# Key-feature sums through one-pass products, and due times shifted by line

## The chip, the cores and the metric

The kernel runs on one core of a Trainium2 chip. The metric is the device time of one execution in microseconds; the time before is the median of three runs, 858.32 us (857.91 to 858.6).

## What is computed

Random-feature attention over q, k, v (4 batches, 8 heads, 576 tokens, head size 64, 128 features) is followed by two feed-forward layers on 2304 tokens of width 512 (inner width 2048), all in fp32:

```python
k_p, q_p = phi(k * scale), phi(q * scale)      # exp of a projection, 128 features
kv  = einsum('bhsm,bhsd->bhmd', k_p, v)
z   = sum(k_p, axis=2)                         # sums of the key features, one row of 128 per head
num = einsum('bhsm,bhmd->bhsd', q_p, kv)
den = einsum('bhsm,bhm->bhs', q_p, z) + 1e-06
x = (num / den) as (2304, 512)
x = leaky_relu(x @ w_in, 0.01) @ w_out
h = x @ w2_in;  out = (h * clip(h + 3, 0, 6) / 6) @ w2_out
```

The change touches z and how it reaches the tokens' denominators.

## The kernel before

**Stages.** Attention works on pairs of heads: 4 batches times 4 pairs give 16 key units (`K_unit`), each followed by query units. Batch 0 stands ahead of everything (`Q_first`, to about 47 us). The other three batches, 12 key units, are woven into the first feed-forward layer (to about 310 us). The second layer runs from there to the end; its products are made by a scheme with fewer multiplications (L1202 for the first product, L1099 for the second).

**Products.** Large products are made of operands cut into a high part and a remainder, both of the type fp32r, in three passes (`mm3`, L520 to L522; also L1099 and L1202). Attention's small products are plain fp32. The scores (L778) use 64 of the array's 128 rows; the products with v (L845) and the numerators (L1002) use 64 of its columns; the transposes (L971, L852) use all of it.

**Sums of the key features.** For batches 1 to 3, `K_unit` adds the 4 blocks of tokens of each head on GpSimd or VectorE (L861 to L866, here L509 and L865 in the profile), which leaves a tile `zr` of 128 partitions by 2 heads by 128 features. One fp32 product with a tile of ones (L869) sums over the partitions and gives every partition the sums; ScalarE or VectorE copies them back to `zr` (L871). The denominators are then taken per token by VectorE against `zr` (L945).

**What sets the order.** Nothing waits at run time to be placed: while the program is built, `Graph.run` plays a list scheduler. Each operation (`g.op`) names the engines that could do it with a cost for each, and a due time; the scheduler takes the one that can start first by its own clock, and among near ones the one that is due first. PE's attention work has three modes, S (64 rows), N (64 columns) and F (whole array), and the constants `WAIT`, `FOLLOW` and `MATE` say how long such work is held back to stand next to its like. The tables `MOVE_A`, `MOVE_W` and `MOVE_R` shift due times of attention units, weights and unpacked weights in steps of 100 ns. Where the scheduler sees PE without work in the first stage it puts in products that nobody reads (`keep_warm`, L1400), 16 of them at the start.

**Tiles.** `h` has 5 buffers (and 6 more in the first stage), `hh` is a small one for a unit of one block, `zr` has 6, `junk` takes an output that nobody reads, `g` is the cut left operand of L1099 (3 buffers, and a fourth, `late_g`, in the second layer).

Of the kernel before, what the change touches and what calls it, by code (L numbers as in the profile page):

```python
# [8 lines left out]
F32 = mybir.dt.float32  # L9
# [28 lines left out]
PACE = 2.215  # L38
WAIT = {"S": 3500.0, "N": 1700.0, "F": 1300.0}
FOLLOW = 200.0  # L40
MATE = 20.0
TURN = {("M", "S"): 193.0, ("M", "N"): 92.0, ("S", "M"): 205.0, ("N", "M"): 158.0, ("F", "S"): 193.0, ("F", "N"): 97.0, ("S", "F"): 175.0,
# [11 lines left out]
ATT = [None, (32000.0, 132000.0), (132e3, 170000.0), (182e3, 244000.0), (220e3, 260000.0)]  # L54
MOVE_A = [[-202, 0, -28, 44, -92, 0, -54, 8, -3],
# [4 lines left out]
MOVE_W = [-30, 30, -3, 103, 35, 68, 105, 97, 0, 53, 7, 110, 0, 28, -99, 0, -14, 35, 50, 3, -192, -42, 60, -500, 41, 288, -17, -51, -123, -27, 96, 0]  # L60
MOVE_R = [24, 10, -139, 36, 14, -45, -29, -31, -102, 77, -175, -71, -46, -9, -4, 0, 59, 11, -146, 0, -17, -36]
RAW = (142000.0, 302000.0)
# [33 lines left out]
class Graph:  # L96
# [17 lines left out]
    def __init__(self):  # L114
        self.ops = []
        self.fifo = {}
        self.todo = {}

    def op(self, alts, rd=(), wr=(), due=0.0, also=(), late=False, lag=0.0, mode="F", after=0.0):
        o = Op()  # L120
        o.phase, o.second = Buf.NOW, Buf.SECOND
        self.todo[o.phase] = self.todo.get(o.phase, 0) + 1
        o.alts, o.due, o.seq, o.lazy = alts, due, len(self.ops), LAZY if late else lag
        o.slack = self.slack if alts[0][0] == "pe" else 0.0
# [242 lines left out]
def attn_moe_kernel(ctx: ExitStack, tc: tile.TileContext, qT, kT, qn, kn, v1, om2, w1i, w1o, w2i, w2o, out):  # L367
# [20 lines left out]
    def many(n, name, *specs, pool=const):  # L388
        return [tuple(sb(f"{name}{i}_{j}", *s, pool=pool) for j, s in enumerate(specs)) for i in range(n)]

    def duo(t, later=0):
# [16 lines left out]
        "sq": many(3, "sq", ([128, 9, 1],), pool=misc),  # L408
        "junk": many(1, "junk", ([128, 2, 128], BF16), pool=misc),
        "hb": [],  # L410
# [10 lines left out]
        "h": many(5, "h", ([128, 512],), pool=right),  # L421
        "hh": many(2, "hh", ([128, 128],), pool=right),
        "ht": many(2, "ht", ([128, 512],), pool=right),
        "tq": many(1, "tq", ([128, 2, 512],), pool=right),
    }
    slots.update(late)
# [60 lines left out]
    wn = sb("wn", [128, 128])  # L487
    ones = sb("ones", [128, 128])
    zero = sb("zero", [128, 128], F32R)
    slots["den"] = many(3, "den", ([128, 4, 1],), ([128, 4, 1],))  # L490
    three = sb("three", [128, 8], pool=misc)[:, 0:1]
    point5 = sb("point5", [128, 32], pool=misc)[:, 0:1]

# [263 lines left out]
    def scores(f, half, xsrc, nsrc, due, nh=1):  # L757
# [8 lines left out]
        ps = [Ps(g.use) for _ in cols]  # L766
        hs = [Buf("h" if c > 1 else "hh") for c in cols]

# [36 lines left out]
    def K_unit(b, hp, due):  # L805
# [49 lines left out]
        for e in range(2):  # L855
            Z = lambda e=e: zr.tiles[0][:, e]

            for i, m in ((1, 256), (0, 128)):
# [7 lines left out]
                 rd=[ht], wr=[(zr, e)], due=due + 3e3)  # L866
        flat = lambda: zr.tiles[0].rearrange("p h m -> p (h m)")
        pz = Ps(g.use)
        g.op([("pe", 435.0, lambda: nc.tensor.matmul(pz.tiles[0][:, 0:256], lhsT=ones, rhs=flat(), start=True, stop=True))],  # L869
             rd=[zr], wr=[pz], due=due + 3.5e3)  # L870
        g.op(copy_alts(flat, lambda: pz.tiles[0][:, 0:256], 256, True), rd=[pz], wr=[zr], due=due + 4e3)  # L871

# [49 lines left out]
    def Q_unit(grp, b, hps, f, half, s0, col0, o, due):  # L922
# [14 lines left out]
        for bank, (h, c) in enumerate(zip(hs, cols)):  # L937
# [4 lines left out]
            def dn(h=h, den=den, jk=jk, heads=heads):  # L942
                for q, (k, _, e) in enumerate(heads):
                    for e, r in [(0, slice(0, 64)), (1, slice(64, 128))] if e is None else [(e, slice(0, 128))]:
                        nc.vector.tensor_tensor_reduce(out=jk.tiles[0][r, q % 2], in0=h.tiles[0][r, q * 128:q * 128 + 128],  # L945
                                                       in1=zr[k].tiles[0][r, e], scale=1.0, scalar=M * EPS, op0=ALU.mult,
                                                       op1=ALU.add, accum_out=den.tiles[0][r, q])
# [437 lines left out]
    with tc.manual_schedule():  # L1385
        nc.vector.memset(three, 3.0)
        nc.gpsimd.memset(ones, 1.0)
        nc.vector.memset(point5, 0.5)
        nc.scalar.activation(slots["nm"][0][0][:, 0], three, AF.Exp)
        nc.sync.dma_start(wn, om2)  # L1390
        nc.gpsimd.memset(zero.bitcast(F32), 0.0)
        make_identity(nc, ident)
        nc.vector.tensor_scalar(out=wn, in0=wn, scalar1=-scale, scalar2=None, op0=ALU.mult)

        def keep_warm(n):
            for _ in range(n):
                nc.tensor.matmul(banks[-1][0][:, 0:384], lhsT=zero[:, 0:128],  # L1400
                                 rhs=zero[:, None, 0:128].to_broadcast([128, 3, 128]), start=True, stop=True)

        g.keep_warm = keep_warm
        g.run(slots, len(banks) - 1, phase, [phase2, phase3, phase4, phase5])
# [81 lines left out]
```

## Time and profile before

| | |
|---|---|
| median of 3 runs | 858.32 us |
| the profiled execution | 858.16 us, span 856.4 us |
| PE busy | 849.2 us of the span |
| DVE, ACT, POOL busy | 658.2, 510.1, 205.0 us |
| DMA | 226 GB/s on average |

The span is the time from the first to the last instruction; the execution's own time is 1.8 us more. PE is TensorE with its products, PEld its loading of weights, DVE is VectorE, ACT is ScalarE, POOL is GpSimd, SP is the engine that issues most DMAs. A product's time in the rows is a latency: two products that follow each other overlap, so the step from one start to the next is what a product occupies.

### The profile page before, as it was taken

The page shows a single profiled execution, that of the slowest core. Times are in us where ns is not written, and L with a number is a line of the kernel's source. Part 1 is how long each engine was busy: PE and PEld are TensorE (multiplying, and loading weights), DVE is VectorE, ACT ScalarE, POOL GpSimd, SP SyncE. Part 2 cuts the span into 40 slices and gives each one's busy share as a digit, 9 for nine tenths or more (in the row PEclk, how much of TensorE's full clock was granted, in tenths as well). Part 3 has the DMA queues.
Part 4 walks back from the last instruction along what each step waited for, and adds up shares of the span by engine and source line. Part 5 has one row for each costly group of instructions (what it writes and reads, how often), then busy time and mean ns, then how long its engine had stood idle before and what let it go on. Part 6 is the DMA issues. An engine that isn't in the chain of part 4 may idle for free.

```text
span 856.4 us, 18060 instructions
## 1 busy us (share of the span) xinstructions
PE 849.2 (99%) x6281; PEld 778.1 (91%) x6281; DVE 658.2 (77%) x1714; ACT 510.1 (60%) x1163; POOL 205.0 (24%) x288
## 2 busy tenths in 40 slices
PE   9999999999999999999999999999999999999998
PEld 8988888889878878888888889999999999999998
DVE  6988998977996855656789757887678779868765
ACT  6988886886887555544654455544543554445432
POOL 0245464334124321000100002122002222422110
PEclk9999999999999999999999999999999999999999
DMA  8666653775757306999878829977896784686451
GB/s 325 221 205 197 216 179 119 244 228 194 234 186 249 126 25 226 321 332 326 327 266 291 284 74 298 314 284 229 297 328 209 237 271 151 193 287 216 155 148 44
DMA packets 110250, 193.83 MB, mean 226 GB/s; under 512 B 13520, under 2 KB 46416, under 8 KB 110160
## 3 DMA queue, kind: packets, MB, share of 16 engines
q1 hardware_dynamic: 110016, 192.55, 68.1%
q8 instruction: 50, 0.82, 0.4%
q14 instruction: 40, 0.33, 0.1%
q10 hardware_dynamic: 144, 0.13, 0.1%
HBM read 148.60 MB, written 44.04 MB: 225 GB/s over the span
## 4 chain that ended last, share of the span: by engine, by line
PE 95%; DVE 2%; ACT 1%; POOL 1%; issue 0%; DVEq 0%; POOLq 0%
PE bank L1099 19%; PE bank L1202 18%; PE bank L520 15%; PE bank L522 15%; PE bank L521 15%; PE bank L778 4%; PE bank L1002 2%; PE bank L845 2%; PE bank L971 1%; PE bank L823 1%; PE bank L897 1%; PE bank L1400 1%; PE bank L869 1%; PE bank L798 0%; PE bank L772 0%
## 5 line engine op out<-in xcount | busy, mean ns | idle before, releaser
L501 ACT COPY late_u<-bank 128x256 f32<-128x256 f32 (+1 forms) x94 | 36.4, 387 | 78.0 <-PE bank L1202 73.8
L1041 DVE TENSOR_TENSOR g<-bank,g 128x512 fp32r<-128x512 f32 (+1 forms) x80 | 50.4, 634 | 39.7 <-ACT g L501 38.7
L1099 PE MATMUL bank<-w,g 128*128 128x256 f32 x612 | 80.8, 275 | 0.0
L1099 PEld LDWEIGHTS bank<-w,g 128*128 128x128 f32 x612 | 74.4, 192 | 0.1
L1202 PE MATMUL bank<-w,late_w 128*128 128x256 f32 x546 | 72.8, 275 | 0.0
L753 ACT ACTIVATE h<-bank,nm 128x128 f32<-128x128 f32 x228 | 63.6, 389 | 10.8 <-DVE nm L747 9.2
L1039 ACT ACTIVATE bank<-bank 128x512 f32<-128x512 f32 (+1 forms) x80 | 44.5, 556 | 41.8 <-PE bank L522 41.7
L1202 PE MATMUL bank<-x,late_w 128*128 128x256 f32 x540 | 69.3, 275 | 0.0
L520 PE MATMUL bank<-x,w 128*128 128x512 f32 (+1 forms) x180 | 67.5, 375 | 0.2 <-DVE g L1041 0.2
L520 PE MATMUL bank<-g,w 128*128 128x512 f32 (+1 forms) x180 | 67.3, 374 | 0.0
L1202 PEld LDWEIGHTS bank<-w,late_w 128*128 128x128 f32 x546 | 67.0, 192 | 0.2
L1202 PEld LDWEIGHTS bank<-x,late_w 128*128 128x128 f32 x540 | 64.9, 192 | 0.2
L522 PE MATMUL bank<-x,w 128*128 128x512 f32 (+1 forms) x180 | 64.6, 359 | 0.0
L521 PE MATMUL bank<-x,w 128*128 128x512 f32 (+1 forms) x180 | 64.5, 358 | 0.0
L521 PE MATMUL bank<-g,w 128*128 128x512 f32 (+1 forms) x180 | 64.5, 358 | 0.0
L522 PE MATMUL bank<-g,w 128*128 128x512 f32 (+1 forms) x180 | 64.5, 358 | 0.0
L741 DVE TENSOR_REDUCE nm<-bank 128x4 f32<-128x512 f32 (+2 forms) x76 | 47.5, 655 | 17.5 <-PE bank L778 15.0
L1099 PE MATMUL bank<-second_w,g 128*128 128x256 f32 x453 | 59.9, 275 | 0.0
L1099 PEld LDWEIGHTS bank<-second_w,g 128*128 128x128 f32 x453 | 55.2, 192 | 0.0
L501 ACT COPY u<-bank 128x256 f32<-128x256 f32 (+1 forms) x59 | 24.0, 409 | 50.0 <-PE bank L1202 30.8
L956 POOL TENSOR_TENSOR h<-h,den 128x512 f32<-128x512 f32 (+2 forms) x32 | 32.9, 1034 | 83.2 <-DVE den L951 52.4
L504 DVE TENSOR_TENSOR g<-xr,g 128x512 fp32r<-128x512 f32 (+1 forms) x55 | 36.7, 667 | 11.8 <-ACT g L501 10.7
(392 smaller groups left out, 2377.5 us busy)
## 6 DMA issues: line engine op xcount, KB each, us to landing
late_w<-in SPq DMA_DIRECT2D x207, 256.0 KB, 4.2
in<-late_w SPq DMA_DIRECT2D x64, 256.0 KB, 3.8
third_w<-in SPq DMA_DIRECT2D x49, 256.0 KB, 4.2
wst<-w2i SPq DMA_DIRECT2D x16, 512.0 KB, 4.5
wst<-w2o SPq DMA_DIRECT2D x16, 512.0 KB, 4.8
x_t<-late_w SPq DMA_DIRECT2D x12, 512.0 KB, 4.4
v<-v SPq DMA_DIRECT2D x14, 330.0 KB, 3.5
wst<-w1i SPq DMA_DIRECT2D x9, 512.0 KB, 3.7
```

Source lines behind the costliest of these rows:

```text
L501: return [("act", c_act(n, psum), lambda: nc.scalar.copy(dst(), src())), dve if psum else dve + (True,)]
L504: return [("dve", c_dve(n), lambda: nc.vector.tensor_tensor(out=dst(), in0=src(), in1=hi().bitcast(F32), op=ALU.subtract), True), ("pool", ...
L520: nc.tensor.matmul(o, lhsT=ah, rhs=bh, start=start, stop=False)
L521: nc.tensor.matmul(o, lhsT=al, rhs=bh, start=False, stop=False)
L522: nc.tensor.matmul(o, lhsT=ah, rhs=bl, start=False, stop=stop)
L741: g.op([("dve", c_dve(c * 128), lambda raw=raw, n_=n_: nc.vector.tensor_reduce(out=n_()[:, :, 0], in_=raw(), axis=AX.X, op=ALU.min))], rd= ...
L753: nc.scalar.activation(h.tiles[0][:, q * 128:q * 128 + 128], raw()[:, q], AF.Exp, bias=nm.tiles[0][:, q], scale=-1.0)
L778: nc.tensor.matmul(ps[e].tiles[0][:, at:at + 128], lhsT=src.tiles[0][r, k * one + i * 128:k * one + i * 128 + 128], rhs=wn[r], start=True, ...
L1039: g.op([("act", c_act(n, True), lambda: nc.scalar.activation(P(), P(), AF.Prelu, alpha=0.01))], wr=[p], due=d)
L1041: g.op([("dve", c_dve(n), lambda: nc.vector.tensor_tensor(out=G1(), in0=P(), in1=G0().bitcast(F32), op=ALU.subtract))], rd=[p, (gg, 0)], w ...
L1099: nc.tensor.matmul(acc[bank].tiles[0][:, half * 256:half * 256 + 256], lhsT=src.tiles[x][:, q * 128:q * 128 + 128], rhs=woven(w[k].tiles[y ...
L1202: nc.tensor.matmul(R[r](), lhsT=w[x], rhs=m[y], start=start and k == n == 0, stop=k == 1 and n == 2, skip_group_check=True)
```

## The change

Four things are done together.

1. The fp32 product with ones (L869) becomes two one-pass products. `zr` is rounded to fp32r in a new tile `zz` (first half, ACT or DVE), the remainder is subtracted into its second half (DVE or POOL), and both are multiplied with ones of the type fp32r into one bank. The moving operand is read in the interleaved order that `woven` gives, so the copy back to `zr` puts the two heads in order again.
2. `ones` is now of type fp32r and also feeds the products of `keep_warm`; the tile `zero` and its fill are gone.
3. `junk` shrinks, `hh` is gone: units of one block take a buffer of `h`.
4. The tables and constants of the order are new, and a table `MOVE_S` shifts due times by the line that calls `g.op`.

```diff
-WAIT = {"S": 3500.0, "N": 1700.0, "F": 1300.0}
-FOLLOW = 200.0
-MATE = 20.0
+WAIT = {"S": 1900.0, "N": 1800.0, "F": 1250.0}
+FOLLOW = 60.0
+MATE = 380.0
...
-MOVE_A = [[-202, 0, -28, 44, -92, 0, -54, 8, -3],
+MOVE_A = [[-369, -68, -26, 0, -91, 0, -38, 0, -69],
...
+MOVE_S = [3, 25, -11, -195, -112, 3, 2, -19, 11, 4, 0, -32, -38, 7, -14, -26, 0, -10, -215, 43, -6, 31, -17, 3, -88, 56, -2, 17, 23, 0, 87, -19, 0, 0, 0, -48, 36, 71, -28, -115, -64, 93, -98, 1, 13, -97, 0, 80, -16, 352, 55, 0, 0, 1, -28, 15, -160, -124, 22, 22, 30, -14, 64, -21, -50, 128, 1, 90, -30, -114, 20, 15, 0, 27, 6, -60, 8, -38, 0, 34, -126, 0, 11]
...
+        self.sites = {}
...
+        site = self.sites.setdefault(sys._getframe(1).f_lineno, len(self.sites))
+        due += MOVE_S[site] * 100.0 if site < len(MOVE_S) else 0.0
...
-        "junk": many(1, "junk", ([128, 2, 128], BF16), pool=misc),
+        "junk": many(1, "junk", ([128, 1, 128], BF16), pool=misc),
...
-        "hh": many(2, "hh", ([128, 128],), pool=right),
...
+        "zz": many(1, "zz", ([128, 512], F32R), pool=right),
...
-    ones = sb("ones", [128, 128])
-    zero = sb("zero", [128, 128], F32R)
+    ones = sb("ones", [128, 128], F32R)
...
-        hs = [Buf("h" if c > 1 else "hh") for c in cols]
+        hs = [Buf("h") for _ in cols]
...
+        zz = Buf("zz")
+        Zh, Zl = (lambda e=e: zz.tiles[0][:, e * 256:e * 256 + 256] for e in range(2))
+        g.op([("act", c_act(256), lambda: nc.scalar.copy(Zh(), flat())), ("dve", 320.0, lambda: nc.vector.tensor_copy(Zh(), flat()), True)],
+             rd=[zr], wr=[(zz, 0)], due=due + 3.2e3)
+        g.op([("dve", c_dve(256), lambda: nc.vector.tensor_tensor(out=Zl(), in0=flat(), in1=Zh().bitcast(F32), op=ALU.subtract), True),
+              ("pool", c_pool(256), lambda: nc.gpsimd.tensor_tensor(out=Zl(), in0=flat(), in1=Zh().bitcast(F32), op=ALU.subtract))],
+             rd=[zr, (zz, 0)], wr=[(zz, 1)], due=due + 3.2e3)
         pz = Ps(g.use)
-        g.op([("pe", 435.0, lambda: nc.tensor.matmul(pz.tiles[0][:, 0:256], lhsT=ones, rhs=flat(), start=True, stop=True))],
-             rd=[zr], wr=[pz], due=due + 3.5e3)
-        g.op(copy_alts(flat, lambda: pz.tiles[0][:, 0:256], 256, True), rd=[pz], wr=[zr], due=due + 4e3)
+        def rep():
+            for n, x in enumerate((Zh, Zl)):
+                nc.tensor.matmul(pz.tiles[0][:, 0:256], lhsT=ones, rhs=woven(x()), start=n == 0, stop=n == 1)
+        g.op([("pe", 224.0, rep)], rd=[zz], wr=[pz], due=due + 3.5e3)
+        back = lambda: zr.tiles[0].rearrange("p h m -> p m h")
+        g.op(copy_alts(back, lambda: pz.tiles[0][:, 0:256].rearrange("p (m h) -> p m h", h=2), 256, True), rd=[pz], wr=[zr], due=due + 4e3)
...
-        nc.gpsimd.memset(ones, 1.0)
+        nc.gpsimd.memset(ones.bitcast(F32), 1.0)
...
-        nc.gpsimd.memset(zero.bitcast(F32), 0.0)
...
-                nc.tensor.matmul(banks[-1][0][:, 0:384], lhsT=zero[:, 0:128],
-                                 rhs=zero[:, None, 0:128].to_broadcast([128, 3, 128]), start=True, stop=True)
+                nc.tensor.matmul(banks[-1][0][:, 0:384], lhsT=ones,
+                                 rhs=ones[:, None].to_broadcast([128, 3, 128]), start=True, stop=True)
```

In the changed kernel's lines, L869 is L883, L865 is L869, L1099 is L1115, L520 to L522 are L524 to L526, L1202 is L1218 and L509 is L513; the new copy is L874 and the new subtraction L877.

**GpSimd, first of the 12 sums.** Names are out<-in; `h1`, `h2` are the key features of the two heads, `ht1` the tail of the batch, `w..` weights being prepared. Before, then the change:

```order
L509 TENSOR_TENSOR h1_0_146<-h1_0_146 128x256
L509 TENSOR_TENSOR h2_0_147<-h2_0_147 128x256
L509 TENSOR_TENSOR zr4_0_138<-h1_0_146 128x128
L509 TENSOR_TENSOR zr4_0_138<-h2_0_147 128x128
L865 TENSOR_TENSOR zr4_0_138<-zr4_0_138,ht1_0_153 64x128 x2
L505 TENSOR_TENSOR w10_93<-wt0_0_110,w10_93 128x512
```

```order
L513 TENSOR_TENSOR h1_0_146<-h1_0_146 128x256
L513 TENSOR_TENSOR h2_0_147<-h2_0_147 128x256
L513 TENSOR_TENSOR zr4_0_138<-h1_0_146 128x128
L513 TENSOR_TENSOR zr4_0_138<-h2_0_147 128x128
L869 TENSOR_TENSOR zr4_0_138<-zr4_0_138,ht1_0_151 64x128 x2
L877 TENSOR_TENSOR zz0_0_153<-zr4_0_138,zz0_0_153 128x256
```

The subtraction of the remainder stands on GpSimd behind the sums, and it does so in all 12 units; its input, the rounded half, comes from ScalarE in 11 of them and from VectorE in one.

**PE, the same sum's product.** Before, then the change (`x..`, `g..` are cut operands of the first layer):

```order
L520 MATMUL bank6_182<-x0_101,w8_91 128x512
L521 MATMUL bank6_182<-x0_101,w8_91 128x512
L522 MATMUL bank6_182<-x0_101,w8_91 128x512
L869 MATMUL bank5_181<-zr4_0_138,ones_186 128x256
L520 MATMUL bank6_182<-x1_102,w8_91 128x512
```

```order
L524 MATMUL bank3_178<-g2_107,w5_88 128x512
L525 MATMUL bank3_178<-g2_107,w5_88 128x512
L526 MATMUL bank3_178<-g2_107,w5_88 128x512
L883 MATMUL bank0_175<-zz0_0_153,ones_185 128x256 x2
L524 MATMUL bank7_182<-g2_107,w5_88 128x512
```

Two instructions stand for one. Between the last product with v of this unit (L845, which frees `h` for the sums) and the product with ones, the order before has 21 one-pass products of 512 columns, the order now 27.

**PE, about 820 us, where the last group's products begin.** Before, `late_g1` is used, refilled and used again:

```order
L1099 MATMUL bank6_182<-w8_91,late_g1_0_0_3824 128x256 x3
L1099 MATMUL bank1_177<-third_w0_0_0_1615,g2_107 128x256 x3
L1099 MATMUL bank3_179<-w4_87,g1_106 128x256 x3
L1099 MATMUL bank4_180<-w3_86,late_g1_0_0_3824 128x256 x3
L1099 MATMUL bank0_176<-w6_89,late_g1_0_0_3824 128x256 x3
L1099 MATMUL bank3_179<-w7_90,late_g1_0_0_3824 128x256 x3
```

Now, at the same place, first products of the next group (L524 to L526) stand between:

```order
L1115 MATMUL bank4_179<-w5_88,g1_106 128x256 x3
L1115 MATMUL bank1_176<-w1_84,g1_106 128x256 x3
L524 MATMUL bank6_181<-x0_101,late_w0_3_0_3921 128x256
L525 MATMUL bank6_181<-x0_101,late_w0_3_0_3921 128x256
L526 MATMUL bank6_181<-x0_101,late_w0_3_0_3921 128x256
L1115 MATMUL bank7_182<-w8_91,g1_106 128x256 x3
L524 MATMUL bank6_181<-x1_102,late_w0_2_0_3920 128x256
L525 MATMUL bank6_181<-x1_102,late_w0_2_0_3920 128x256
L526 MATMUL bank6_181<-x1_102,late_w0_2_0_3920 128x256
L1115 MATMUL bank4_179<-w6_89,late_g1_0_0_3922 128x256 x3
```

Before, 6 products stand between the last use of the buffer's old content and the first use of its new one; now 18 do (three L524 to L526 ahead of the first row shown are the rest of them).

## Rows read from the trace of the kernel before

**Rows 1.** The page: engines' busy time, and the chain that ended last, by engine

```profile
PE 849.2 (99%) x6281; PEld 778.1 (91%) x6281; DVE 658.2 (77%) x1714; ACT 510.1 (60%) x1163; POOL 205.0 (24%) x288
...
PE 95%; DVE 2%; ACT 1%; POOL 1%; issue 0%; DVEq 0%; POOLq 0%
```

**Rows 2.** Stretches: length, then PE, PEld, DVE, ACT, POOL busy, clock, DMA

```profile
68.00:140.00 72.00, 71.77 (x424) 60.53 (x423) 65.75 (x135) 58.57 (x126) 36.90 (x38) 1.00 0.58 188
...
300.00:480.00 180.00, 180.00 (x879) 154.05 (x879) 127.54 (x272) 97.90 (x194) 15.74 (x16) 1.00 0.79 269
```

**Rows 3.** Timeline of PE around the first product with ones: start, length, instruction

```profile
69.62 0.38 PE L522 MATMUL bank<-x,w 128*128 128x512 f32 x1
69.83 0.59 PE L869 MATMUL bank<-zr,ones 128*128 128x256 f32 x2
70.08 0.57 PE L520 MATMUL bank<-x,w 128*128 128x512 f32 x1
70.48 0.38 PE L521 MATMUL bank<-x,w 128*128 128x512 f32 x1
```

**Rows 4.** Timeline of PE: one-pass products of 256 columns

```profile
152.41 0.28 PE L521 MATMUL bank<-x,w 128*128 128x256 f32 x1
152.52 0.28 PE L522 MATMUL bank<-x,w 128*128 128x256 f32 x1
```

**Rows 5.** Timeline of PE around the fourth product with ones

```profile
131.66 0.38 PE L522 MATMUL bank<-g,second_w 128*128 128x512 f32 x1
132.04 0.70 PE L869 MATMUL bank<-zr,ones 128*128 128x256 f32 x2
...
132.80 0.38 PE L521 MATMUL bank<-g,second_w 128*128 128x512 f32 x1
```

**Rows 6.** Timeline of PE: into the 64-row scores and out again

```profile
143.36 0.38 PE L522 MATMUL bank<-g,second_w 128*128 128x512 f32 x1
143.67 0.94 PE L778 MATMUL bank<-wn,xT 64*128 64x128 f32 x12
144.54 0.88 PE L971 MATMUL bank<-ident,h 128*128 128x128 f32 x6
```

**Rows 7.** Groups by form, ACT and POOL: count, busy us, mean ns, idle before

```profile
L501 ACT CAST late_w<-late_u 128x256 fp32r<-128x256 f32 x9 | 3.6, 405 | 0.8 <-DMA in<-late_w 0.5 <-DVE late_u L508 0.3
...
L505 POOL TENSOR_TENSOR x<-xr,x 128x256 fp32r<-128x256 f32 x5 | 3.7, 742 | 0.1
```

**Rows 8.** Timeline of PE, 717 to 719.6 us

```profile
717.51 1.35 PE L1099 MATMUL bank<-w,g 128*128 128x256 f32 x9
719.01 0.60 PE L1099 MATMUL bank<-third_w,g 128*128 128x256 f32 x3
```

**Rows 9.** Timeline, 821.5 to 825.5 us: the refill of `late_g`, then PE's next products

```profile
822.89 0.51 ACT L501 CAST late_g<-xr 128x384 fp32r<-128x384 f32 x1 [2.31 <-PE bank L1099]
...
823.44 0.84 DVE L504 TENSOR_TENSOR late_g<-xr,late_g 128x384 fp32r<-128x384 f32 x1
...
823.46 0.38 PE L1099 MATMUL bank<-w,late_g 128*128 128x256 f32 x1
...
824.34 1.16 PE L1099 MATMUL bank<-w,late_g 128*128 128x256 f32 x8 [0.50 <-DVE late_g L504]
```

**Rows 10.** Timeline of the first stage: the start, and a VectorE operation beside GpSimd

```profile
0.87 0.20 POOL L1391 MEMSET zero<- 128x128 f32 x1
...
1.13 5.49 PE L1400 MATMUL bank<-zero 128*128 128x384 f32 x16 [1.13 <-POOL zero L1391]
...
39.05 0.68 DVE L560 SCALAR_TENSOR_TENSOR wst<-wt,wst 128x512 uint32<-128x512 uint32 x1
...
44.74 1.29 POOL L505 TENSOR_TENSOR w<-first_wt,w 128x512 fp32r<-128x512 f32 x1
44.77 1.37 PEld L1400 LDWEIGHTS bank<-zero 128*128 128x128 f32 x8
44.80 1.67 PE L1400 MATMUL bank<-zero 128*128 128x384 f32 x8
...
45.52 1.06 DVE L560 SCALAR_TENSOR_TENSOR wst<-first_wt,wst 128x512 uint32<-128x512 uint32 x1
...
46.50 0.41 DVE L906 TENSOR_TENSOR u<-bank,den 128x256 f32<-128x256 f32 x1
...
46.97 0.66 PE L915 MATMUL bank<-ident,u 128*128 128x128 f32 x4 [0.51 <-DVE u L906]
```

More of the change, by code (lines that the diff above doesn't have):

```diff
@@ L1 @@
+import sys
 from contextlib import ExitStack
@@ L54 @@
 ATT = [None, (32000.0, 132000.0), (132e3, 170000.0), (182e3, 244000.0), (220e3, 260000.0)]
-MOVE_A = [[-202, 0, -28, 44, -92, 0, -54, 8, -3],
[4 rows of a table removed]
-MOVE_W = [-30, 30, -3, 103, 35, 68, 105, 97, 0, 53, 7, 110, 0, 28, -99, 0, -14, 35, 50, 3, -192, -42, 60, -500, 41, 288, -17, -51, -123, -27, 96, 0]
-MOVE_R = [24, 10, -139, 36, 14, -45, -29, -31, -102, 77, -175, -71, -46, -9, -4, 0, 59, 11, -146, 0, -17, -36]
+MOVE_A = [[-369, -68, -26, 0, -91, 0, -38, 0, -69],
[4 rows of a table added]
+MOVE_W = [-95, 4, -18, 11, 0, 63, 106, 113, -32, 76, 0, 0, -47, -18, 0, 20, -2, 7, 35, -114, -233, 48, 108, -735, -22, 116, 113, 71, -62, -128, 0, 8]
+MOVE_R = [8, 43, -131, 71, -104, 0, -42, -39, -108, 115, 0, 103, -15, 99, -26, 0, -18, -83, -20, -282, 0, 69]
+MOVE_S = [3, 25, -11, -195, -112, 3, 2, -19, 11, 4, 0, -32, -38, 7, -14, -26, 0, -10, -215, 43, -6, 31, -17, 3, -88, 56, -2, 17, 23, 0, 87, -19, 0, 0, 0, -48, 36, 71, -28, -115, -64, 93, -98, 1, 13, -97, 0, 80, -16, 352, 55, 0, 0, 1, -28, 15, -160, -124, 22, 22, 30, -14, 64, -21, -50, 128, 1, 90, -30, -114, 20, 15, 0, 27, 6, -60, 8, -38, 0, 34, -126, 0, 11]
 RAW = (142000.0, 302000.0)
@@ L487, in attn_moe_kernel @@
     wn = sb("wn", [128, 128])
-    ones = sb("ones", [128, 128])
-    zero = sb("zero", [128, 128], F32R)
+    ones = sb("ones", [128, 128], F32R)
     slots["den"] = many(3, "den", ([128, 4, 1],), ([128, 4, 1],))
     three = sb("three", [128, 8], pool=misc)[:, 0:1]
-    point5 = sb("point5", [128, 32], pool=misc)[:, 0:1]
+    point5 = sb("point5", [128, 8], pool=misc)[:, 0:1]
     def Ps(use):
@@ L944, in dn @@
                     for e, r in [(0, slice(0, 64)), (1, slice(64, 128))] if e is None else [(e, slice(0, 128))]:
-                        nc.vector.tensor_tensor_reduce(out=jk.tiles[0][r, q % 2], in0=h.tiles[0][r, q * 128:q * 128 + 128],
+                        nc.vector.tensor_tensor_reduce(out=jk.tiles[0][r, 0], in0=h.tiles[0][r, q * 128:q * 128 + 128],
                                                        in1=zr[k].tiles[0][r, e], scale=1.0, scalar=M * EPS, op0=ALU.mult,
```

8 rows, old and new, of the table MOVE_A are left out of this document.

## The prediction

> **What bounds the kernel now.** I read the page first, for who is busy and which chain ended last. PE is busy for 849.2 of 856.4 us and makes up 95% of the chain [rows 1]. A busy PE is not yet a PE without gaps, because a product's length in the rows is a latency; so the view by stretches came next, and then the timeline of PE, where the step from one start to the next is what a product occupies. In the stretches PE shows no idle time from 300 to 480 us and 0.2 us from 68 to 140 [rows 2]. In the timeline the steps are 0.21 us for 512 columns [rows 3] and 0.11 us for 256 [rows 4], and after 50 us they leave these values in a few places only. So the kernel's time is the sum of PE's steps, plus a few waits, plus a first stage (to about 47 us) in which PE is held up by a chain through ScalarE and VectorE, plus a short end. Work that leaves PE shortens the kernel one for one, if nothing else becomes late.
>
> **The product with ones.** Before, it stands between two products of 512 columns. From its start at 69.83 to the start of the second product behind it at 70.48 are 0.65 us; one 512-column step of 0.21 is in that, so the fp32 product occupies 0.44 us [rows 3]. Now two one-pass products of 256 columns stand there, at 0.11 each [rows 4]: 0.22 us, with the same interleaved reading that those of rows 4 have. The saving is a little over 0.21 us, 12 times: **-2.5 us**. What could make it less is a loading of ones that isn't hidden; each 256-column product of rows 4 loads its own weights too and keeps its step, so I take no such cost.
>
> **What it adds elsewhere.** Per sum one rounding of 256 columns, on ScalarE in 11 of 12 cases, 0.41 us by the nearest row, and one subtraction of 256 columns on GpSimd, 0.74 us by the nearest row [rows 7]. Together that is 4.5 us on ScalarE (11 of them) and 8.9 us on GpSimd, over some 220 us. Neither is on PE's path by itself. But the chain from the last product with v to the product with ones becomes longer by 0.41 + 0.74 = 1.15 us and two hand-overs. It is covered if the order leaves PE that much more to do in between. It does: counted in the order at the steps of rows 3 and 4, PE's work between the two is 4.8 to 8.5 us before and 6.1 to 9.4 now; the first has 6 more products of 512 columns, 1.3 us. Only the third has 6.1 us in both. Before, one of the twelve made PE wait, the fourth: it started 0.38 us after its predecessor instead of 0.21, and its own stretch took 0.76 instead of 0.65, together 0.28 us lost [rows 5]. If the third now does what the fourth did, the extra link costs at most 1.15 us there; if the fourth is on time (9.4 us of work now), 0.28 come back. I take 0 for both.
>
> **Changes of the array's shape.** A step into the 64-row scores is 0.31 us where 0.21 would do, 0.10 lost, and the way out costs some more [rows 6]. That is what `FOLLOW`, `MATE` and `WAIT` trade in. Counted over both orders, scores stand in 34 runs before and now, and 64-column products in 28; but pairs of the two that stand side by side go from 15 to 14, so there is one more change of shape in all, 109 to 110. **+0.2 us**, between 0.1 and 0.3.
>
> **The order late in the program.** Two places lose time to PE waiting on its own refills. At 717.51 nine products of 256 columns take 1.50 us to the next start, where nine steps are 1.01: 0.49 lost [rows 8]. At 823.46 one product takes 0.88 us instead of 0.11: 0.77 lost [rows 9]. The second is plain to read: `late_g1` may be refilled only when the products that read it are through; the cast on ScalarE starts at 822.89 and takes 0.51, the subtraction on VectorE starts at 823.44 and takes 0.84, and PE has just 6 products, 0.67 us, in between. In the order now 18 products, 2.0 us, stand there, and the cast and the subtraction need 0.51 + 0.84 = 1.35. At the place that answers to 717 us, products of the next group are likewise put between. I take both waits as gone: **-1.3 us**, between -1.6 (smaller ones beside them vanish too) and 0 (they turn up at the next refill).
>
> **The first stage.** The fill of `zero`, 0.20 us, goes, and the opening run of 16 unread products, which waited for it until 1.13 us, can start up to 0.2 us earlier [rows 10]. There are 39 unread products instead of 37, at about 0.2 us each by the run of 8 at 44.80 [rows 10]; they stand where the scheduler saw nothing to do, and I cost them at nothing, since PE would wait there anyway; without that cover they are +0.4. The products at the chain's end keep their order, and the VectorE operation at 45.52 (L560) still stands ahead of the last multiplication of that stage (L906 at 46.50), on which the last transposes wait (L915 at 46.97) [rows 10]. I take 0, between -0.6 and +0.8.
>
> **The middle, 50 to 310 us.** Every attention unit stands at another place than before. The waits there are small: I found none larger than the 0.28 at the fourth sum [rows 5], and four or five such, about 1 us in all, are the most that can be won; new ones may come. I take 0, between -1 and +1.5. DMAs are issued in another order too; the core's 16 engines are 0.58 to 0.79 busy in the stretches that I read [rows 2], and I cost that at nothing.
>
> **Sum.** The profiled execution took 858.16 us: 858.16 - 2.5 + 0.2 - 1.3 = 854.56. The median of the runs is 0.16 above that execution, less than the terms are known to. I predict **854.6 us**.
>
> **The rivals.**
> - *Only the products count.* The late waits stay or come back at other refills: 858.16 - 2.5 + 0.2 = 855.9. For it: such waits depend on 0.1 us, and VectorE's queue can delay a refill with enough PE work beside it. Against it: 2.0 us stand where 1.35 are needed.
> - *The saving is eaten by new waits in the middle.* The longer chain to the product with ones misses its place a few times, or other units wait: the third at 1.15 us and as much again at others, 855.9 + 1.2 = 857.1, no change that can be told. For it: VectorE is busy for 65.75 of 72 us from 68 to 140 [rows 2], so there is little room. Against it: eleven of twelve distances grew.
> - *GpSimd's new work blocks VectorE: slower.* A VectorE operation that takes 0.68 us (39.05) takes 1.06 at 45.52, where a subtraction on GpSimd from 44.74 for 1.29 overlaps its start [rows 10]. So 12 more GpSimd subtractions of 0.74 can push VectorE back by up to 8.9 us in all; where its room is used up (6.25 us are left from 68 to 140, with four of the sums), PE waits for the cut operands `g`. With all of it landing on PE, 854.6 + 8.9 = 863.5; it decides from 5.3 us landed, which turns -3.6 into +1.7. The Trainium skill, "SBUF — State Buffer", section "SBUF: two separate sides", says that GpSimd and VectorE share a port pair under an exclusive lock, held for a whole instruction; by that rule the loser stands still for as long as the other still needs. The trace agrees: the 0.38 us added to L560 lie inside GpSimd's 1.29. Against it: each block lasts under a microsecond, and where VectorE is fullest PE was idle for 0.2 us in all [rows 2].
> - *The one-pass products don't keep their step*, because ones are loaded in a way that rows 4 don't show, and take as long as the fp32 one: 854.6 + 2.5 = 857.1.
>
> **How the numbers follow.** My forecast, up to 0.9 us to either side of 854.6: 0.50. Only the products count, 855.4 to 856.6: 0.28. Better than forecast, because waits in the middle and the first stage go as well (854.6 - 1 - 0.6 = 853.0 and about): 0.06. Saving eaten or steps not kept, within 0.2% of 858.3 (1.7 us, about what a measurement of this kernel can tell from no change): 0.13. Slower: 0.03. So faster 0.84, same 0.13, slower 0.03. The range is 853.0 to 857.3: down to where the middle and the first stage both pay, up over the eaten saving; outside are some 0.05 below and 0.09 above.
>
> **What would show it.** In the changed kernel's profile: 24 products on L883 as pairs, 0.22 us from the first start to the product behind the pair; about 849.2 - 3.6 us of PE busy time; no gap over 0.3 us on PE near 715 and 820 us; VectorE's share not above 78%. The prediction is wrong if PE waits for `zz` (L877) by name more than once or twice, if VectorE's operations beside L877 grow and PE waits behind them, or if the first stage ends more than 0.8 us away from where it did (the last L915 started at 46.97 us).

## The result, and the profile after

The changed kernel takes 863.73 us, the median of 4 runs (863.36 to 865.65), where the kernel before takes 858.29: a ratio of 1.0065, with a 95% interval of 1.0052 to 1.0079. It is slower by 5.4 us. The forecast was 854.6, faster. The profiled execution took 865.65 us, span 863.9, the longest of the four, so it shows about 2 us more loss than the median.

The places that the prediction named (the pair, the two late waits) came as it said; PE's busy time fell by 0.4 us, not by 3.6. From the page of the changed kernel, busy time, and the chain that ended last by engine and by line:

```profile
PE 848.8 (98%) x6283; PEld 776.0 (90%) x6283; DVE 658.7 (76%) x1720; ACT 520.6 (60%) x1183; POOL 206.3 (24%) x285
...
PE 78%; DVE 8%; DMA 5%; ACT 4%; issue 2%; POOL 1%; SPq 0%; DVEq 0%; ACTq 0%; POOLq 0%
PE bank L1115 19%; PE bank L1218 17%; PE bank L524 11%; PE bank L526 11%; PE bank L525 11%; DMA wst<-w2i 2%; PE bank L782 2%; DVE junk L961 2%; ACT h L757 1%; DMA xn<-qn 1%; DVE nm L745 1%; DVE wst L564 1%; DVE g L1057 1%; PE bank L827 1%; 
```

The chain is 78% PE where it was 95% [rows 1]; the rest of it runs through other engines. PE itself is idle for 15.1 us of the span (863.9 less 848.8), where it was for 7.2 (856.4 less 849.2). Timeline of PE, the first product with ones and the place that answers to [rows 8]:

```profile
70.74 0.38 PE L526 MATMUL bank<-g,w 128*128 128x512 f32 x1
70.96 0.38 PE L883 MATMUL bank<-zz,ones 128*128 128x256 f32 x2
71.18 0.38 PE L524 MATMUL bank<-g,w 128*128 128x512 f32 x1
...
718.34 1.17 PE L1115 MATMUL bank<-second_w,g 128*128 128x256 f32 x9
719.35 1.50 PE L1115 MATMUL bank<-second_w,late_g 128*128 128x256 f32 x12
720.69 1.17 PE L1115 MATMUL bank<-second_w,g 128*128 128x256 f32 x9
```

The pair takes 0.22 us from its start to the next product, where the fp32 product took 0.44 [rows 3]. Nine products take 1.01 us to the next start (718.34 to 719.35), as nine steps should, where [rows 8] had 1.50; the wait of [rows 9] has no counterpart either. The loss is in the middle. The view by stretches, 80 to 340 us (length, then PE, PEld, DVE, ACT, POOL busy, clock, DMA share, GB/s), before:

```profile
80.00:340.00 260.00, 259.77 (x1856) 218.69 (x1855) 210.03 (x635) 192.66 (x494) 96.67 (x118) 1.00 0.57 183
```

The same of the change, and whom PE waited for there:

```profile
80.00:340.00 260.00, 251.91 (x1814) 210.90 (x1813) 206.33 (x616) 189.95 (x483) 102.87 (x131) 1.00 0.53 168
```

```profile
PE bank L883 <- ACT h L757: 1.6, 1, 1.6
PE bank L782 <- DVE g L1057: 1.5, 1, 1.5
PE bank L526 <- DVE g L1057: 1.2, 1, 1.2
PE bank L524 <- ACT xr L505: 0.8, 1, 0.8
PE bank L524 <- DVE g L1057: 0.8, 1, 0.8
```

PE is idle for 8.1 us there in place of 0.2, in eleven waits, nearly all for ScalarE and VectorE; the five longest are shown. The first, at the seventh product with ones, is not one for `zz`: that sum's `zz` was finished 4.5 us before the product started. One small wait for `zz` there is, at the third sum, and this view leaves it out. The second product of the pair needs the end of the subtraction, and the next product starts 0.70 us after the start of the pair, where the same place takes 0.32 without the subtraction (115.51 to 115.83 in the run without it, below):

```profile
116.80 0.73 POOL L877 TENSOR_TENSOR zz<-zr,zz 128x256 fp32r<-128x256 f32 x1 [0.52 <-ACT zz L874]
117.10 0.86 PE L883 MATMUL bank<-zz,ones 128*128 128x256 f32 x2
117.80 0.38 PE L524 MATMUL bank<-g,second_w 128*128 128x512 f32 x1
```

VectorE's busy time in this stretch is *lower* than before, with 616 instructions in place of 635; over the whole span it is the same (658.7 and 658.2 us). What it does in its idle time shows in its timeline. Before, reductions of one query unit against `zr`, each with a reading of its accumulator:

```profile
215.19 0.28 DVE L945 CUSTOM_DVE_ANT_0 junk<-h,zr 128x128 bf16<-128x128 f32 x1
215.40 0.08 DVE L945 DVE_READ_ACCUMULATOR2_ANT den<- 128x1 f32 x1
215.40 0.29 DVE L945 CUSTOM_DVE_ANT_0 junk<-h,zr 128x128 bf16<-128x128 f32 x1
215.61 0.08 DVE L945 DVE_READ_ACCUMULATOR2_ANT den<- 128x1 f32 x1
215.63 0.29 DVE L945 CUSTOM_DVE_ANT_0 junk<-h,zr 128x128 bf16<-128x128 f32 x1
```

And in the change:

```profile
218.16 0.28 DVE L961 CUSTOM_DVE_ANT_0 junk<-h,zr 128x128 bf16<-128x128 f32 x1
218.37 0.08 DVE L961 DVE_READ_ACCUMULATOR2_ANT den<- 128x1 f32 x1
218.48 0.29 DVE L961 CUSTOM_DVE_ANT_0 junk<-h,zr 128x128 bf16<-128x128 f32 x1
218.70 0.08 DVE L961 DVE_READ_ACCUMULATOR2_ANT den<- 128x1 f32 x1
218.93 0.29 DVE L961 CUSTOM_DVE_ANT_0 junk<-h,zr 128x128 bf16<-128x128 f32 x1
```

Before, a reduction starts 0.21 us after the last one, before that one's 0.28 are over. Now it starts 0.32 or 0.45 after it, always behind its end, and so do all 102 that follow another directly. The change cut `junk`, the output that nobody reads, from two halves used in turn to one. It made room, and the prediction passed over it. This theory came only after the first four runs, which all kept the short `junk`.

### The profile page after: what moved, and what is told of

It reads as the page before. It is cut to its first block, busy times and chain, and to the rows that moved or that the text cites. A ratio compares the mean times of both kernels' runs of the same rounds, so it can differ in the third digit from the quotient of the medians.

```text
span 863.9 us, 18057 instructions
## 1 busy us (share of the span) xinstructions
PE 848.8 (98%) x6283; PEld 776.0 (90%) x6283; DVE 658.7 (76%) x1720; ACT 520.6 (60%) x1183; POOL 206.3 (24%) x285
## 4 chain that ended last, share of the span: by engine, by line
PE 78%; DVE 8%; DMA 5%; ACT 4%; issue 2%; POOL 1%; SPq 0%; DVEq 0%; ACTq 0%; POOLq 0%
PE bank L1115 19%; PE bank L1218 17%; PE bank L524 11%; PE bank L526 11%; PE bank L525 11%; DMA wst<-w2i 2%; PE bank L782 2%; DVE junk L961 2%; ACT h L757 1%; DMA xn<-qn 1%; DVE nm L745 1%; DVE wst L564 1%; DVE g L1057 1%; PE bank L827 1%; PE bank L913 1%
## 5 line engine op out<-in xcount | busy, mean ns | idle before, releaser
L1115 PE MATMUL bank<-w,g 128*128 128x256 f32 x594 | 81.9, 275 | 0.0
L1218 PE MATMUL bank<-x,late_w 128*128 128x256 f32 x558 | 74.7, 275 | 0.0
L1115 PEld LDWEIGHTS bank<-w,g 128*128 128x128 f32 x594 | 73.9, 192 | 0.0
L1218 PE MATMUL bank<-w,late_w 128*128 128x256 f32 x540 | 71.1, 275 | 0.0
L1218 PEld LDWEIGHTS bank<-x,late_w 128*128 128x128 f32 x558 | 68.5, 192 | 0.3 <-ACT late_u L505 0.2
L524 PE MATMUL bank<-x,w 128*128 128x512 f32 (+1 forms) x180 | 66.6, 370 | 1.8 <-ACT xr L505 0.8
L1218 PEld LDWEIGHTS bank<-w,late_w 128*128 128x128 f32 x540 | 66.1, 192 | 0.5 <-ACT late_u L505 0.2
L524 PE MATMUL bank<-g,w 128*128 128x512 f32 (+1 forms) x180 | 66.1, 367 | 0.0
L526 PE MATMUL bank<-x,w 128*128 128x512 f32 (+1 forms) x180 | 64.8, 360 | 0.1
L526 PE MATMUL bank<-g,w 128*128 128x512 f32 (+1 forms) x180 | 64.5, 358 | 0.0
L1115 PE MATMUL bank<-second_w,g 128*128 128x256 f32 x438 | 60.0, 275 | 0.0
L1115 PEld LDWEIGHTS bank<-second_w,g 128*128 128x128 f32 x438 | 54.4, 192 | 0.0
L961 DVE CUSTOM_DVE_ANT_0 junk<-h,zr 128x128 bf16<-128x128 f32 (+1 forms) x128 | 43.6, 341 | 10.3 <-ACT h L757 1.2
L505 ACT CAST g<-xr 128x384 fp32r<-128x384 f32 (+1 forms) x47 | 26.4, 562 | 30.6 <-PE bank L1115 15.8
```

The source lines that it names most:

```text
L505: return [("act", c_act(n, psum), lambda: nc.scalar.copy(dst(), src())), dve if psum else dve + (True,)]
L524: nc.tensor.matmul(o, lhsT=ah, rhs=bh, start=start, stop=False)
L526: nc.tensor.matmul(o, lhsT=ah, rhs=bl, start=False, stop=stop)
L961: nc.vector.tensor_tensor_reduce(out=jk.tiles[0][r, 0], in0=h.tiles[0][r, q * 128:q * 128 + 128], in1=zr[k].tiles[0][r, e], scale=1.0, sca ...
L1115: nc.tensor.matmul(acc[bank].tiles[0][:, half * 256:half * 256 + 256], lhsT=src.tiles[x][:, q * 128:q * 128 + 128], rhs=woven(w[k].tiles[y ...
L1218: nc.tensor.matmul(R[r](), lhsT=w[x], rhs=m[y], start=start and k == n == 0, stop=k == 1 and n == 2, skip_group_check=True)
```

## The experiments

"New order" is the change's, "old order" that of before; unless said otherwise the instructions stand row for row as there. Times are medians, ratios against runs of the kernel before on the same chip (857.96 to 858.29 us). Theories: **A**, the new order makes loads late; **B**, the longer chain to the product with ones holds PE; **C**, GpSimd's subtractions hold VectorE; **D**, `junk`.

### Four runs with the short junk

New order (with the tables, the tile `ones` and the buffers of `h` as in the change), fp32 product, no rounding and no subtraction:

```diff
-g.op([("act", c_act(256), lambda: nc.scalar.copy(Zh(), flat())), ...
+g.op([("act", c_act(256), lambda: None), ...
...
-    nc.tensor.matmul(pz..., lhsT=ones, rhs=woven(x()), start=n == 0, stop=n == 1)
+    nc.tensor.matmul(pz..., lhsT=ones.bitcast(F32), rhs=flat(), start=True, stop=True)
```

> The changed kernel's order on every engine, row for row, with the fp32 product with ones in place of the two one-pass ones, and without the rounding (L874) and the subtraction (L877). Theory A (the new order as such: ScalarE waits for loads that land after their readers' turn, and PE waits behind it): the loss between 80 and 340 us stays at about 11 us of PE time, the products cost 2.5 more, so 863.7 + 2.5 = 866 us, and not under 864.5. Theory B (the longer chain to the product with ones holds PE): the chain is as before again, the gaps go, 858 to 861. Theory C (GpSimd's subtractions hold VectorE by their shared port, 8.9 us in all): they are gone, so 863.7 - 8.9 + 2.5 = 857 to 858.

861.90 us, ratio 1.0044 (1.0031 to 1.0057): none of the three. B and C are not all of it, and A's 866 is missed by 4.

Old order, one-pass products, rounding and subtraction on GpSimd, one half of `junk`; the remainder is left out of the sums:

```diff
+nc.gpsimd.tensor_copy(Zh(), flat())
+nc.gpsimd.tensor_tensor(out=flat(), in0=flat(), in1=Zh().bitcast(F32), op=ALU.subtract)
...
+for n, x in enumerate((Zh, Zh)): nc.tensor.matmul(pz..., lhsT=ones, rhs=woven(x()), ...)
```

> The order of the kernel before, row for row, with one-pass products of 256 columns with ones; rounding and subtraction both stand on GpSimd behind the last addition of a sum (twice the new GpSimd work of the change, 24 instructions of about 0.74 us). Both products read the high part, so the remainder is left out of the sums. Theory A: nothing else is late, 858.3 - 2.5 = 855.8, between 855.3 and 856.8. Theory B: PE waits for the high part at several of the twelve sums, 857 to 860. Theory C: twice the subtractions, 858.3 - 2.5 + 17 = 873, and in any case more than 858.

869.41 us, ratio 1.0134 (1.0119 to 1.0150). A falls: the order is that of before, and 11 us are lost.

The change, with short loads of raw weights:

```diff
-nc.sync.dma_start(st..., src[j])
+n = 1024 if st.slot not in SEEN else 32
+nc.sync.dma_start(st...[:, 0:n], src[j][:, 0:n])
```

> The changed kernel, its order row for row, but each load of raw weights (L542, 512 KB) after the first into its buffer brings only 32 of 1024 columns; the weights that they should bring are left out, all else runs as it did. Theory A: the loads land in time, ScalarE's waits for wst go (about 10 of 15 us between 85 and 300), and PE's loss in the middle of 11 us falls to 2 to 6: 855 to 860 us. Theories B and C: the gaps are not made by loads, so no change, 863 to 864.

862.63 us, ratio 1.0052 (1.0039 to 1.0064): 1.1 us back, a difference within the intervals of the two. ScalarE's waits for `wst` are gone, and the DMA engines' share from 80 to 340 us is 0.32 in place of 0.53:

```profile
80.00:340.00 260.00, 255.94 (x1830) 214.65 (x1829) 207.41 (x619) 191.78 (x487) 104.48 (x132) 0.99 0.32 96
```

PE still stands idle for 4.1 us there (8.1 in the change's slowest run). Late loads are a small part of the loss at most: with two halves of `junk` (below) ScalarE still waits 5.7 us for `wst`, and PE idles for 1.5 us in this stretch.

The change's program with the old numbers for the order (a third order):

> The changed program (rounding, subtraction, one-pass products, as in the change) with the numbers of before for the order (WAIT, FOLLOW, MATE, the three MOVE tables) and none by line. The planner knows the new operations, so the order is a third one, near that of before. Theory A: the loss depends on whether loads come late in this order, which its numbers were not set for: 856 to 862. Theory B and C: it has the new chain and the new GpSimd work as the change has, 862 to 865.

879.98 us, ratio 1.0247 (1.0233 to 1.0262), outside all expectations. The short `junk` is in it, which alone costs the order of before 9.9 us (below); what makes the rest stays open. That the planner's numbers fit one program only is a guess.

### junk

Two halves again in the change (256 bytes, taken from unused columns of `g`), one half in the kernel before, and two halves in the first two kernels above:

```diff
-"junk": many(1, "junk", ([128, 1, 128], BF16), pool=misc),
+"junk": many(1, "junk", ([128, 2, 128], BF16), pool=misc),
...
-out=jk.tiles[0][r, 0]
+out=jk.tiles[0][r, q % 2]
```

> The changed kernel, row for row, with the scratch tile junk of two halves again, used in turn as before (the room comes from unused columns of the g tiles). Theory D: with one half each reduction on L961 waits for the writes of the one before it, and follows it after 0.324 us instead of 0.213 (medians of the trace of the change and of before), 0.11 us more some 145 times, 16 us on VectorE's queue in a stretch where it had little room; PE waits behind it for g, nm and den. So two halves take back most of the 9 to 11 us that the middle loses: 854.6 to 858. Theories A, B and C (order and loads, longer chain, GpSimd's port): junk has nothing to do with it, 863 to 864.

858.29 us, ratio 1.0006 (0.9997 to 1.0015): 5.4 us come back, in the same order. D's range ended at 858: the sign is right, the size fell short of it by 0.3.

> The kernel before, row for row, with junk of one half as in the change, and nothing else. Theory D: 0.11 us more at each of some 145 reductions in an order that was set for two halves: 861 to 868 us. Theories A, B and C: no change, 858.3.

867.96 us, ratio 1.0113 (1.0099 to 1.0127): this one edit costs the kernel before 9.9 us.

> The new order with the fp32 product (as in the run with the order alone) and with two halves of junk. Theory D: the order by itself costs nothing in the middle and takes away the late waits, 858.3 - 1.3 + 0.2 = 857.2, between 856.5 and 858.5. Theory A: the order itself makes the loads late, 861.5 to 862 as with one half.

857.20 us, ratio 0.9991 (0.9982 to 1.0000), as D said: the new order, with all else in the change but `junk` and the products, is no worse than the old.

> The order of before with the one-pass products, rounding and subtraction on GpSimd, and two halves of junk; the second product reads the high part again, so the remainder is left out. Theory D: most of the 11 us above before go; 855.8 if the longer chain fits into the old order, up to 860 if it doesn't (theory B: its fourth sum was late already before). Theory C: 24 new operations on GpSimd still hold VectorE, 864 and more.

859.13 us, ratio 1.0014 (1.0005 to 1.0023): 10 of the 11 us went with `junk`; what is left is below.

Of the four theories only D has all four signs. The view by lines of VectorE's instructions (count, busy us, mean ns, then idle time ahead of them) in the kernel before, the change, the change with two halves, and before with one half:

```profile
L945 DVE CUSTOM_DVE_ANT_0 junk<-h,zr 128x128 bf16<-128x128 f32 (+1 forms) x128 | 44.6, 387 | 1.3 <-ACT h L753 0.6
```

```profile
L961 DVE CUSTOM_DVE_ANT_0 junk<-h,zr 128x128 bf16<-128x128 f32 (+1 forms) x128 | 43.6, 341 | 10.3 <-ACT h L757 1.2 <-ACT tq L505 0.2
```

```profile
L961 DVE CUSTOM_DVE_ANT_0 junk<-h,zr 128x128 bf16<-128x128 f32 (+1 forms) x128 | 40.2, 351 | 2.0 <-ACT h L757 1.2
```

```profile
L945 DVE CUSTOM_DVE_ANT_0 junk<-h,zr 128x128 bf16<-128x128 f32 (+1 forms) x128 | 50.8, 397 | 9.5 <-ACT h L753 0.8 <-ACT g L501 0.5 <-DVE den L945 0.2
```

With one half VectorE idles for about 10 us ahead of these reductions, and other engines are named for 1.4 of it. In the change 8.8 of the 10.3 us are gaps of under 0.15 us each, for which this view names nobody. The records of the instructions do: 100 of the 128 reductions wait for a semaphore that VectorE's own instructions raise, with two halves 44; in the old order 82 with one half, 23 with two. The expectations' count of 145 and the medians 0.213 and 0.324 took waiting records along. Counted over the timeline alone, there are 128 reductions, and 102 follow another directly in the new order: these steps add up to 45.2 us with one half and 33.1 with two, 12 us of VectorE's queue, and with one half none is under 0.30 us, with two 50 are under 0.25. In the old order 96 follow directly, and the steps add up to 49.1 us with one half, 29.1 with two.

### What is left of the miss: 3.7 us

All of these are the change with two halves, with one thing more taken away or moved. First the rounding and subtraction done for nobody, beside the fp32 product:

```diff
-nc.gpsimd.tensor_tensor(out=Zl(), in0=flat(), in1=Zh().bitcast(F32), ...)
+nc.gpsimd.tensor_tensor(out=Zl(), in0=Zh().bitcast(F32), in1=Zh().bitcast(F32), ...)
...
+nc.tensor.matmul(pz..., lhsT=ones.bitcast(F32), rhs=flat(), start=True, stop=True)
```

> The new order with two halves of junk and the fp32 product (857.2 us before these edits), and with the rounding (L874) and the subtraction (L877) in their places, but with nobody waiting for what they write: the subtraction takes the high part from itself, the product reads the sum as before. Theory C (GpSimd's subtraction holds VectorE by their port; the trace with two halves has 5.3 us of VectorE operations lengthened beside L877): the 3.6 us that rounding and subtraction cost beyond the -2.5 are here too, 859 to 861. Theory B (the longer chain, PE waits for the product's operands): nothing on PE's path has changed, 857.2 to 857.8.

860.59 us, ratio 1.0026 (1.0015 to 1.0037), 3.4 us above the new order without them (3.0 by the ratios). C, not B. Not all of it need be VectorE beside the subtractions: between 55 and 310 us, where these stand, the profiled execution is 2.3 us longer than the one without them, and 1.0 more is a wait far behind the last of them:

```profile
546.74 0.94 PE L1218 MATMUL bank<-w,third_w 128*128 128x256 f32 x6 [1.03 <-DVE xr L1256]
```

No subtraction (`lambda: None` in its place, and `(Zh, Zh)` as the operands):

> The changed kernel with two halves of junk (858.3 us), without the twelve subtractions; the second one-pass product reads the high part again, so the remainder is left out. The chain has the rounding (0.41 us) only. Theory C: the port is free, 857.2 - 2.5 = 854.7, up to 855.5. Theory B: a third of the longer chain stays, so a third of the 3.6 us: 855.9; from this run alone B and C aren't told apart, from it and the one with nobody waiting they are.

856.97 us, ratio 0.9984 (0.9976 to 0.9993): 1.3 us back (1.9 by the ratios), 2.3 above C's 854.7 and 1.5 above the end of its range.

The subtraction as `nc.vector.tensor_tensor`:

> The changed kernel with two halves of junk (858.3 us), the twelve subtractions on VectorE in place of GpSimd, at the same place of the program. Each takes about 0.35 us of VectorE's queue (4 us in all) instead of 5.3 us of lengthening, and the chain is 0.4 us shorter. Theory C: about 1 us comes back, 857 to 858. Theory B: a third of the cost comes back too, 857; if VectorE has to wait in its queue for the rounding on ScalarE, 859 and more.

858.19 us, ratio 1.0000 (0.9991 to 1.0009): no gain. VectorE now makes the subtractions itself, 0.42 us each by the median, 5 us in all, and stands idle for 4.3 us ahead of three of them, for the rounding. That its queue pays either way is how I read it.

Then the parts one by one, for a theory **E** as well: the roundings hold up ScalarE's queue. The products read `ones` in place of `zz`, and rounding, subtraction or both are `None`:

> The changed kernel with two halves of junk (858.3 us), without rounding and subtraction; the one-pass products read the ones themselves and wait for no sum, so the sums over tokens are left out. If the products are worth what the forecast says: 857.2 - 2.5 = 854.7, between 854 and 855.5. If they are not: 856 and more.

856.73 us, ratio 0.9981 (0.9972 to 0.9990): by the expectation, less than the forecast said. The pair takes 0.24 us in these four runs in place of 0.22, so their products save 0.2 us less than those of the change.

> As the run with the products alone, with the twelve roundings (L874) in their places behind the last addition of their sum; nobody waits for them, and the sums are left out as there. Theory E (ScalarE's queue: eleven roundings of 0.41 us and about 2 us of waiting for the sum, in a stretch where much waits for ScalarE): 1.5 to 2.5 us more than with the products alone. Theories B and C: no more than 0.3.

856.66 us, ratio 0.9978 (0.9969 to 0.9987): the rounding costs nothing. E falls.

> As the run with the roundings, but they read the constant matrix ident, and so wait for no sum (left out as there). If the waiting in ScalarE's queue is what costs, the time is that of the products alone; if the length does (4.5 us of ScalarE), that of the run with the roundings.

856.08 us, ratio 0.9972 (0.9963 to 0.9981): the same within its interval.

> As the run with the products alone, with the twelve subtractions on GpSimd (and no roundings), of ident from itself, waited for by nobody and waiting for nothing; the sums are left out as there. Theory C: they lengthen VectorE's operations by some 5 us, and 1.3 us or more of it comes out at the end. Theories B and E: no more than 0.3 us more than with the products alone.

858.42 us, ratio 0.9999 (0.9990 to 1.0008), 1.7 us above the products alone, with subtractions that nobody waits for: C. In the timeline of the change with two halves, VectorE and GpSimd around one subtraction:

```profile
133.65 0.73 POOL L877 TENSOR_TENSOR zz<-zr,zz 128x256 fp32r<-128x256 f32 x1
133.71 1.22 DVE L567 SCALAR_TENSOR_TENSOR wt<-wt,wst 128x512 uint32<-128x512 uint32 x1
```

L567 has a median of 0.68 us; here it takes 1.22. Over the twelve subtractions VectorE's operations beside them are 4.6 us longer than the medians of their lines and shapes.

Last, one product per sum, on the high part alone, without rounding's remainder:

```diff
-for n, x in enumerate((Zh, Zl)):
+for n, x in enumerate((Zh,)):
```

> The changed kernel with two halves of junk, no subtraction, and one product of 256 columns with ones per sum: the high part alone; the remainder of about one part in some thousand is left out of the sums. PE has 12 x 0.11 = 1.3 us less to do than with two products (857.0). If time taken off PE comes out one for one: 855.7; if VectorE and ScalarE set the pace in that stretch: 856.3 to 857.

855.36 us, ratio 0.9964 (0.9951 to 0.9978). 1.3 us leave PE, by the steps at the twelve sums, and 1.6 come out (1.7 by the ratios, uncertain by 1.4 each way): as much as expected, within what can be told. This is faster than both kernels; its sums hold the high part only.

## Why the prediction was wrong

In ratios to the kernel before, the forecast was 0.9958 and the result 1.0065: 0.0107 apart, 9.2 us.

- **`junk`: a term that was never in the sum, 5.1 us** (1.0065 to 1.0006). The diff showed it, front and rows had all that was needed: [rows 2] gave VectorE 6.25 free us in 72, and I wrote myself "there is little room". The step that failed is "The middle, 50 to 310 us ... I take 0, between -1 and +1.5": it listed what moves and left out what VectorE must do longer. The same argument that I applied to GpSimd's subtractions, that VectorE's queue is nearly full, decides here too. The Trainium skill, "VectorE: DVE Perf Modes", section "The DRAIN you can't avoid", says that the next operation can't start before the pipeline is empty and that "the semaphore costs nothing extra here"; by that the cut would be free. The trace differs: with two halves a reduction starts 0.21 us after one that lasts 0.28, and forbidding that costs 9.9 us in the old order. The section's remark that an operation that is not held starts earlier agrees with the 0.21.
- **GpSimd blocks VectorE: the rival was right in kind, priced too high, and given too small a chance.** Not 8.9 us landed but, by the ratios, 1.5 (the subtractions alone), 1.9 (the run without them) and 3.0 (the idle pair, which holds the roundings and the wait at 546 us too); 1.0006 with it against 0.9979, the mean of the four runs without, is 2.3 us. Its price of 863.5 met the result by chance. The Trainium skill, "SBUF — State Buffer", section "SBUF: two separate sides", has the two engines exclude each other for a whole instruction; L567 beside L877 agrees (1.22 us in place of 0.68; the 0.54 added lie inside L877's 0.73).
- **The late waits: right.** Both are gone in the change, and the new order with the fp32 product and two halves gives 0.9991, where its terms (+0.2, -1.3) give 0.9987. The +0.2 has no run of its own.
- **The product with ones: the step was right, not all of its gain reached the end.** Added over the twelve sums, from the start of the product to that of the second product behind it are 7.77 us with the fp32 product (new order, two halves) and 5.26 with the pair (no subtraction): 2.5 us, as forecast. In the times, 0.9991 to 0.9979 are 1.0 us; with rounding and subtraction on both sides, 1.0026 to 1.0006 are 1.7. Either is uncertain by about 1 us. The traces don't decide it: between 55 and 310 us the four runs without the subtraction are 1.8 to 3.3 us shorter than the fp32 run, but that one was profiled in an execution 1.7 us above its median. How much of the 1.5 that is missing is waits that move in, and how much scatter, stays open.
- **The longer chain: rightly 0, and the places were right.** The third sum does wait for the subtraction, as feared: 0.37 us in the change, 0.45 with two halves, in place of at most 1.15. The fourth, which lost 0.28 before [rows 5], is on time. Rounding for nobody costs nothing. In the old order with one half the wait was 1.5 us at the fourth sum, so that the new order gives the chain room is right too.
- **The first stage: rightly 0.** The last of its transposes starts at 47.18 us, before at 47.35; the 46.97 that the prediction took from [rows 10] is the first of four. Executions of the same instructions (the fp32 run and the four without the subtraction) differ by up to 1.3 us before 55 us, where nothing was changed.
- **PE's busy time: the sign was wrongly set.** It took the late waits off busy time, though PE is in part idle in them, and a product that stands alone counts as busy for 0.38 us where its step is 0.21 [rows 3].
- **DMAs at nothing: right in the end.** Their waits grew, but short loads gave back 1.1 us only, within the intervals.

The sum: 5.1 + 2.3 + 1.5 + 0.3 (the order, 0.9991 against 0.9987) = 9.2. The 5.1 are uncertain by 1.4; by the idle pair the next two would be 3.0 and 0.8.

## What to carry to other kernels

Read every line of a diff for what it takes from the queue that is fullest, the lines that only make room first of all: an output that nobody reads is still a tile that two instructions write in turn, and one copy of it serialises them. An engine that idles ahead of its own instructions shows in no busy share; compare the step from start to start of the same instruction in both traces before a theory on order or loads. When two changes come in one edit, take the order row for row from one side and the other part from the other; a third order, made by planning anew with old numbers (880 us here), tells nothing of either.

## What the runs showed that I had not expected

- Two reductions on VectorE overlap by 0.07 us when their outputs differ (0.21 from start to start, 0.28 long), and are 0.30 us or more apart, mostly up to 0.45, when they share an output: 12 us over 102 pairs in the new order, 20 over 96 in the old. VectorE waits there for its own semaphore.
- The engine whose queue held things up had its busy share fall, from 77% [rows 1] to 76%.
- Taking 31 of every 32 columns from the largest loads changed the time by 0.1% (1.1 us, within the intervals), though ScalarE had waited some 10 us for them.
